# Fourteen steps of a two-part cached attention kernel written as a hardware loop of seven iterations

## Chip, cores and metric

The kernel runs on one core of a Trainium2 chip. The metric is the time of one execution in microseconds (us), as the device measures it. Several runs are made and their median is given.

## What is computed

Two attentions over a cache, A and B, each for one new token and 32 heads of 128 numbers, with 16384 cached positions per head. A looks at all positions, B only at the last 4096. Each multiplies its result by an output matrix, and the two results are put side by side.

```python
def _A_ref(x, k_cache, v_cache, wq, wo):      # B: the same over the last W = 4096 positions
    q = (x @ wq).reshape(B, Sq, Hq, Dh)       # one query row per head, 32 heads of 128
    scores = einsum("bhqd,bhkd->bhqk", q, k) * (Dh ** -0.5)
    p = softmax(scores)
    o = einsum("bhqk,bhkd->bhqd", p, v)
    return o.reshape(B, Sq, Hq * Dh) @ wo     # 4096 numbers times a 4096 x 512 matrix
...
return concatenate([a, b], axis=-1)
```

Nearly all bytes are the two caches: 352.32 MB are read from HBM in one execution.

## The kernel before, in words

**Steps.** The work is cut into 20 steps, and each step handles one tile of K and one tile of V. A tile is 128 partitions of 256 positions of 128 bf16 numbers, 8.39 MB. A step of A takes two heads (64 partitions each). A step of B takes two groups of four heads, loaded as two halves. There are 16 steps of A and 4 of B; B stands at the steps 0, 7, 13 and 19. A Python loop (`for T in range(NT)`, L446 and on) writes all 20 steps out one after the other, so the program is straight-line code.

**What a step does.** Scores are made on DVE: the K tile is multiplied by the query in place (`scores_prod`, L227), halves of the products are added until eight numbers per position are left (`scores_tree`, L233), and these are reduced (L237). That is done for both halves of the tile, and then `unit_max` takes the maximum (L244), which PE transposes into PSUM (L249). The rest of a step's work is done inside the next step, between its DVE instructions: `max_all` (DVE L262 and L264, PE L268), the exponentials on ACT (`soft`, L276 and L282; `spread_p`, L297), their sum on PE (L315), the product with V on PE (`pv`, 64 matmuls of 512 columns, L331), scaling on ACT (`evict`, L340), four small matmuls (`columns`, L348), and a copy into the collected output by ACT (L352).

**Buffers.** Two slots hold K tiles (`kring`) and one slot holds V tiles (`vring`). So the load of V for step T-1 can start only when the matmuls of `pv` of step T-2 have read the slot, and the load of K for step T+1 only when DVE has finished step T-1.

**Order.** `manual_schedule` keeps the instructions of each engine in the order in which they are written. All loads of K, V and the weights are issued by SP, in this order within step T: V of step T-1 (L132 for A, L141 for B), then K of step T+1 (L117 for A, L123 for B). An issue that has to wait holds up the issues behind it. The tail after the last step loads the second half of the last V tile and the output weights of B in five pieces (L141, L157), projects A's output (L383) and then B's (L397).

Of the kernel before, what the change touches and what calls it, by code (L numbers as in the profile page):

```python
# [11 lines left out]
P = 128  # L12
# [13 lines left out]
def kernel(  # L26
# [24 lines left out]
    singles = ctx.enter_context(tc.tile_pool(name="singles", bufs=1))  # L51
    kring = ctx.enter_context(tc.tile_pool(name="kring", bufs=2))
    vring = ctx.enter_context(tc.tile_pool(name="vring", bufs=1))
    small = ctx.enter_context(tc.tile_pool(name="small", bufs=3))
# [3 lines left out]
    ps_o = ctx.enter_context(tc.tile_pool(name="ps_o", bufs=1, space=bass.MemoryType.PSUM))  # L58
    ps_m = ctx.enter_context(tc.tile_pool(name="ps_m", bufs=2, space=bass.MemoryType.PSUM))

    def kslot(name):
        return kring.tile([P, 2 * CH, DH], BF16, tag="kring", name=name)

    def vslot(name):
        return vring.tile([P, 2 * CH, DH], BF16, tag="vring", name=name)

# [24 lines left out]

    steps, na, nb = [], 0, 0
    for T in range(HQ // 2 + HQ // 8):
        if T in (0, 7, 13, 19):
            steps.append((B, nb))
            nb += 1
        else:
            steps.append((A, na))
            na += 1
    NT = len(steps)  # L100
    assert na == HQ // 2 and nb == HQ // 8

    K, V = {}, {}

    def b_window(cache, g):
        return cache[0, 4 * g : 4 * g + 4, SkB - WB : SkB, :].rearrange("h (i l) d -> i h (l d)", l=CH)

    def a_pair(cache, g):
        return cache[0, 2 * g : 2 * g + 2, :, :].rearrange("h (i l) d -> (h i) l d", l=2 * CH)

    def new_k(T):
        K[T] = kslot("kt")

    def load_k(T, u=None):
        s, g = steps[T]
        if s is A:
            nc.sync.dma_start(  # L117
                out=K[T][:, :, :].rearrange("p l d -> p (l d)"),
                in_=a_pair(A_k_cache, g).rearrange("p l d -> p (l d)"),
            )  # L120
        else:
            for v in (0, 1) if u is None else (u,):
                nc.sync.dma_start(  # L123
                    out=K[T][:, v * CH : (v + 1) * CH, :].rearrange("p l d -> p (l d)"),
                    in_=b_window(B_k_cache, 2 * g + v),
                )

    def load_v(T):
        s, g = steps[T]
        V[T] = vslot("vt")  # L130
        if s is A:
            nc.sync.dma_start(  # L132
                out=V[T][:, :, :].rearrange("p l d -> p (l d)"),
                in_=a_pair(A_v_cache, g).rearrange("p l d -> p (l d)"),
            )
        else:
            for u in (0, 1):
                load_v_half(T, u, V[T][:, u * CH : (u + 1) * CH, :])

    def load_v_half(T, u, dst):  # L140
        nc.sync.dma_start(  # L141
            out=dst.rearrange("p l d -> p (l d)"), in_=b_window(B_v_cache, 2 * steps[T][1] + u)
        )

# [63 lines left out]

    class Unit:
        def __init__(self, T):  # L210
            self.T = T
            self.s, self.g = steps[T]
            self.n = 2 * CH // self.s.parts
            self.rows = 4 * self.s.nh
            self.last = T == NT - 1
            self.sc = one.tile([P, 2 * CH], F32, tag="sc", name="sc")

        def col(self, v):
            return self.s.nh * (self.s.parts * self.g + v)

    units = {}

    def scores_prod(T, u):
        s, g = steps[T]
        k = K[T][:, u * CH : (u + 1) * CH, :]
        j = g if s is A else 2 * g + u
        nc.vector.tensor_tensor(out=k, in0=k, in1=s.q[:, j : j + 1, :].broadcast_to([P, CH, DH]), op=ALU.mult)  # L227

    def scores_tree(T, u):
        k = K[T][:, u * CH : (u + 1) * CH, :]  # L230
        w = DH // 2
        while w >= 8:
            nc.vector.tensor_tensor(out=k[:, :, 0:w], in0=k[:, :, 0:w], in1=k[:, :, w : 2 * w], op=ALU.add)  # L233
            w //= 2
        if u == 0:
            units[T] = Unit(T)
        nc.vector.tensor_reduce(  # L237
            out=units[T].sc[:, u * CH : (u + 1) * CH], in_=k[:, :, 0:8], axis=AX.X, op=ALU.add
        )

    def unit_max(un):
        n = un.s.parts
        m = small.tile([P, 2], F32, tag="m", name="m")
        nc.vector.tensor_reduce(  # L244
            out=m[:, 0:n], in_=un.sc[:, :].rearrange("p (v l) -> p v l", v=n), axis=AX.X, op=ALU.max
        )
        un.sm = ps_m.tile([P, 512], F32, tag="sm", name="sm")
        for v in range(n):
            nc.tensor.transpose(un.sm[0:1, v * P : (v + 1) * P], m[:, v : v + 1], identf[:, :])  # L249
# [75 lines left out]
    def pv(un):  # L325
        s, n, G = un.s, un.n // 4, un.s.groups
        for i in range(n):
            for v in range(s.parts):
                r0 = 32 * (v * G + i % G)
                l = v * n + i  # L330
                nc.tensor.matmul(  # L331
                    s.o[r0 : r0 + un.rows, :],
                    lhsT=un.pm[:, l, :, :].rearrange("p a b -> p (a b)"),
                    rhs=V[un.T][:, 4 * l : 4 * l + 4, :],
                    start=(i < G), stop=(i >= n - G),
                )
# [5 lines left out]
    def columns(un):  # L342
        s = un.s
        w = s.parts * s.nh
        oc = ps_s.tile([P, 8], F32, tag="sp", name="oc")
        sel = s.sel[:, :, :].rearrange("k v (h c) -> k c (v h)", c=4)
        for j in range(4):
            nc.tensor.matmul(  # L348
                oc[:, 0:w], lhsT=un.osb[:, j * P : (j + 1) * P], rhs=sel[:, j, :],
                start=(j == 0), stop=(j == 3),  # L350
            )
        nc.scalar.copy(s.O[:, un.col(0) : un.col(0) + w], oc[:, 0:w])  # L352

    def pv_columns(un, v, V_t):
        s = un.s
        oc = ps_s.tile([P, 4], F32, tag="sp", name="ocol")
        for l in range(un.n):
# [4 lines left out]
        nc.vector.tensor_tensor(  # L362
            out=s.O[:, un.col(v) : un.col(v) + s.nh], in0=oc[:, :],
            in1=un.r[:, v * s.nh : (v + 1) * s.nh], op=ALU.mult,
# [25 lines left out]
    def project_out_columns(s, pieces):  # L390
# [19 lines left out]
        nc.sync.dma_start(out=out[0, 0, DN : 2 * DN].rearrange("(c f) -> c f", c=nf), in_=rows[:, :])  # L410

    wo_pieces = (16, 8, 4, 3, 1)
    with tc.manual_schedule():
        scratch = kslot("scratch")
        x0 = 4 * KC * P
        for s in (B, A):
            s.x_row = scratch[0:1, :, :].rearrange("p a b -> p (a b)")[:, x0 : x0 + D]
            for a, b in ((0, D // 4), (D // 4, D // 2), (D // 2, D)):
                nc.scalar.dma_start(out=s.x_row[:, a:b], in_=s.x[0, 0:1, a:b])  # L419
            x0 += D  # L420
        new_k(0)
        wqt = vslot("wqt")
        load_wq(B, wqt[:, 0:CH, :])
        load_k(0, 0)
        load_wq(A, wqt[:, CH : 2 * CH, :])
        load_k(0, 1)
        make_identity(nc, identf[:, :])
# [5 lines left out]
        nc.vector.tensor_copy(ident[:, :], identf[:, :])  # L433
        spread_x(B, scratch[:, :, :].rearrange("p a b -> p (a b)"))
        for s in (B, A):
# [7 lines left out]
        project_q(A)  # L443
        new_k(1)
        load_k(1)
        for T in range(NT):  # L446
            if T >= 1:
                load_v(T - 1)
                if T + 1 < NT:
                    new_k(T + 1)  # L450
                    load_k(T + 1)
            if T == NT - 1:
                W = kslot("wot")
                load_wo(A, W[:, 0:CH, :], (HQ,))
                load_v_half(T, 0, W[:, CH : 2 * CH, :])
            scores_prod(T, 0)
            if T >= 1:
                un = units[T - 1]
                max_all(un)
                soft(un)  # L460
                spread_p(un)
                soft_sum(un)
                pv(un)
            scores_tree(T, 0)
            if T >= 1:
                recip(un)
                evict(un)
                columns(un)
            scores_prod(T, 1)
            scores_tree(T, 1)  # L470
            if T < NT - 1:
                unit_max(units[T])
        Z = vslot("wot")
        load_v_half(NT - 1, 1, Z[:, 0:CH, :])
        load_wo(B, Z[:, CH : 2 * CH, :], wo_pieces)
        un = units[NT - 1]
        permute_o(A)
        project_out_rows(A)
# [7 lines left out]
        pv_columns(un, 0, W[:, CH : 2 * CH, :])  # L486
        pv_columns(un, 1, Z[:, 0:CH, :])
        permute_o(B)
# [31 lines left out]
```

## Time and profile before

| | us |
|---|---|
| median of 3 runs (825.7 to 826.01) | 825.76 |
| span of the profiled execution | 823.9 |
| outside the span (difference to the median) | 1.9 |
| DVE busy in the span | 763.9 (93%) |
| PE busy, matmuls | 202.7 (25%) |
| ACT busy | 60.1 (7%) |
| DMA queue q1, share of 16 engines | 99.2% |
| bytes read from HBM | 352.32 MB, 428 GB/s over the span |

The span is one profiled execution from the first instruction to the last. A share of busy time tells how much of the span an engine worked. It does not tell that the engine sets the end: that is read from the waits and from the chain of work that ended last. The DMA share is the mean over the 16 DMA engines that carry this core's transfers, counted as the time that their packets took. The line numbers of the rows are those of the kernel before.

### The profile page before, as it was taken

To read this page: it belongs to the slowest core of one execution; us is meant where nothing else is said; L and a number is where in the kernel's file an instruction comes from. 1 tells how busy PE (TensorE), PEld (TensorE's weight loads), DVE (VectorE), ACT (ScalarE), POOL (GpSimd) and SP (SyncE) were. 2 spreads that over 40 slices of the span, in tenths; PEclk is the share of its full clock that TensorE was granted. 3 is DMA by queue.
4 is the path that set the end of the run, shared out by engine and by line. 5 is a ranking of instruction groups with operands and counts; after the bars stand their busy time and mean duration, and the time that the engine had idled before them with its cause. 6 is when DMAs were issued, how large, how long until landed. Compare 5 with 4: busy or idle time off the path is not lost.

```text
span 823.9 us, 4724 instructions
## 1 busy us (share of the span) xinstructions
PE 202.7 (25%) x1985; PEld 100.7 (12%) x1985; DVE 763.9 (93%) x353; ACT 60.1 (7%) x168; POOL 0.7 (0%) x6
## 2 busy tenths in 40 slices
PE   2702212203030303130312213030303020303175
PEld 0201100101010101010101101010101010101035
DVE  2899999999999999999999999999999999999980
ACT  0101000001010000100000000010100000000010
POOL 0000000000000000000000000000000000000000
PEclk9865656565565555565555565565656565556585
DMA  9999999999999999999999999999999999999997
GB/s 384 434 433 433 453 420 443 430 436 440 423 446 420 424 439 443 412 453 420 443 417 449 414 452 410 450 417 428 438 449 424 436 433 430 443 414 445 418 429 296
DMA packets 8107, 352.62 MB, mean 428 GB/s; under 512 B 915, under 2 KB 1046, under 8 KB 1302
## 3 DMA queue, kind: packets, MB, share of 16 engines
q1 hardware_dynamic: 8072, 352.33, 99.2%
q8 instruction: 15, 0.25, 0.1%
q14 instruction: 6, 0.05, 0.0%
q10 hardware_dynamic: 14, 0.00, 0.0%
HBM read 352.32 MB, written 0.00 MB: 428 GB/s over the span
## 4 chain that ended last, share of the span: by engine, by line
DMA 82%; PE 15%; DVE 1%; SPq 0%; issue 0%; ACTq 0%; ACT 0%; DVEq 0%
DMA vt<-in_A_v_cache_dram 65%; DMA vt<-in_B_v_cache_dram 13%; PE oA L331 11%; DMA wot<-in_B_wo_dram 4%; PE oB L331 2%; PE qp L203 2%; DMA scratch<-in_A_x_dram 2%; DVE kt L227 1%; SPq L141 0%; ACTq L419 0%; SPq L157 0%; PE out_cols L397 0%; ACT qB L207 0%; PE out_rows L407 0%; DVE rows L409 0%
## 5 line engine op out<-in xcount | busy, mean ns | idle before, releaser
L233 DVE TENSOR_TENSOR kt<-kt 128x8192 bf16<-128x8192 bf16 (+3 forms) x160 | 344.9, 2156 | 4.8
L227 DVE TENSOR_TENSOR kt<-kt,qA 128x16384 bf16<-128x16384 bf16 x32 | 277.8, 8683 | 11.0 <-DMA kt<-in_A_k_cache_dram 10.9
L331 PE MATMUL oA<-vt,pm 128*8 128x512 bf16 x1024 | 92.3, 538 | 132.1 <-DMA vt<-in_A_v_cache_dram 132.1
L227 DVE TENSOR_TENSOR kt<-kt,qB 128x16384 bf16<-128x16384 bf16 x8 | 69.4, 8680 | 6.3 <-ACT qB L207 6.3
L249 PE MATMUL sm<-identf,m 128*1 128x128 f32 x24 | 8.1, 370 | 227.3 <-DVE m L244 227.3
L331 PEld LDWEIGHTS <-pm 128*8 128x8 bf16 (+1 forms) x1216 | 37.3, 111 | 216.7 <-issue 196.3
L268 PE MATMUL sm<-one_f,Mr 1*128 1x1 f32 x48 | 12.9, 347 | 176.7 <-DVE Mr L264 147.1
L237 DVE TENSOR_REDUCE sc<-kt 128x128 f32<-128x1024 bf16 x40 | 48.8, 1220 | 2.7
L276 ACT ACTIVATE bias<-sm 128x1 f32<-128x1 f32 (+1 forms) x20 | 3.4, 172 | 420.8 <-PE sm L268 420.8
L268 PEld LDWEIGHTS sm<-one_f,Mr 1*128 1x128 f32 x48 | 11.2, 298 | 183.6 <-DVE Mr L264 152.2
L249 PEld LDWEIGHTS sm<-identf,m 128*1 128x1 f32 x24 | 1.7, 79 | 229.3 <-issue 216.2
L340 ACT ACTIVATE o<-oA,r 128x512 f32<-128x512 f32 x16 | 11.0, 688 | 220.5 <-PE oA L331 220.5
L331 PE MATMUL oB<-vt,pm 128*16 128x512 bf16 x192 | 17.2, 494 | 20.3 <-DMA vt<-in_B_v_cache_dram 16.2
L348 PE MATMUL oc<-selA,o 128*128 128x2 f32 x128 | 16.9, 254 | 12.7 <-ACT o L340 12.7
L348 PEld LDWEIGHTS oc<-selA,o 128*128 128x128 f32 x128 | 15.5, 191 | 20.8 <-ACT o L340 20.8
L297 ACT ACTIVATE pm<-p,maskA 128x256 bf16<-128x256 bf16 x32 | 14.5, 500 | 0.5
L315 PE MATMUL sm<-cs,rowsA 128*128 128x1 f32 x32 | 9.4, 362 | 14.3 <-ACT p L282 14.3
L282 ACT ACTIVATE p<-sc,bias 128x256 bf16<-128x256 f32 (+1 forms) x24 | 11.3, 470 | 0.6
L203 PE MATMUL qp<-wqt,xbA 128*128 128x512 bf16 x32 | 8.8, 444 | 6.0 <-DVE kt L227 6.0
L315 PEld LDWEIGHTS sm<-cs,rowsA 128*128 128x128 f32 x32 | 8.0, 310 | 15.7 <-ACT p L282 15.7
L203 PE MATMUL qp<-wqt,scratch 128*128 128x512 bf16 x32 | 9.9, 486 | 0.0
L362 DVE TENSOR_TENSOR OB<-ocol,r 128x4 bf16<-128x4 f32 x2 | 0.3, 161 | 10.2 <-PE ocol L358 10.2
(71 smaller groups left out, 108.1 us busy)
## 6 DMA issues: line engine op xcount, KB each, us to landing
kt<-in_B_k_cache_dram SPq DMA_DIRECT2D x8, 4096.0 KB, 29.1
vt<-in_B_v_cache_dram SPq DMA_DIRECT2D x6, 4096.0 KB, 23.3
wot<-in_B_v_cache_dram SPq DMA_DIRECT2D x2, 4096.0 KB, 22.6
wqt<-in_B_wq_dram SPq DMA_DIRECT2D x1, 4096.0 KB, 12.3
wqt<-in_A_wq_dram SPq DMA_DIRECT2D x1, 4096.0 KB
wot<-in_A_wo_dram SPq DMA_DIRECT2D x1, 4096.0 KB
wot<-in_B_wo_dram SPq DMA_DIRECT2D x1, 2048.0 KB
wot<-in_B_wo_dram SPq DMA_DIRECT2D x1, 1024.0 KB
```

What stands on the lines that cost most here:

```text
L203: nc.tensor.matmul(qp[:, :, :], lhsT=s.xb[:, j, c, :], rhs=wq[:, c, j, g : g + 4, :], start=(k == 0), stop=(k == n - 1),)
L227: nc.vector.tensor_tensor(out=k, in0=k, in1=s.q[:, j : j + 1, :].broadcast_to([P, CH, DH]), op=ALU.mult)
L233: nc.vector.tensor_tensor(out=k[:, :, 0:w], in0=k[:, :, 0:w], in1=k[:, :, w : 2 * w], op=ALU.add)
L237: nc.vector.tensor_reduce(out=units[T].sc[:, u * CH : (u + 1) * CH], in_=k[:, :, 0:8], axis=AX.X, op=ALU.add)
L249: nc.tensor.transpose(un.sm[0:1, v * P : (v + 1) * P], m[:, v : v + 1], identf[:, :])
L268: nc.tensor.matmul(un.sm[:, 256 + v : 257 + v], lhsT=Mr[:, v * P : (v + 1) * P], rhs=one_f[:, :], start=True, stop=True,)
L282: nc.scalar.activation(out=un.p[:, v * n : (v + 1) * n], in_=un.sc[:, v * n : (v + 1) * n], func=ACT.Exp, scale=inv, bias=bias[:, v : v + ...
L297: nc.scalar.activation(out=out, in_=in_, func=ACT.Copy, scale=mask)
L315: nc.tensor.matmul(un.sm[v * w : (v + 1) * w, 264:265], lhsT=s.rows[:, :, :, :].rearrange("p r a b -> p (r a b)"), rhs=un.cs[:, v : v + 1] ...
L331: nc.tensor.matmul(s.o[r0 : r0 + un.rows, :], lhsT=un.pm[:, l, :, :].rearrange("p a b -> p (a b)"), rhs=V[un.T][:, 4 * l : 4 * l + 4, :], ...
L340: nc.scalar.activation(out=un.osb[:, :], in_=un.s.o[:, :], func=ACT.Copy, scale=un.r[:, 0:1])
L348: nc.tensor.matmul(oc[:, 0:w], lhsT=un.osb[:, j * P : (j + 1) * P], rhs=sel[:, j, :], start=(j == 0), stop=(j == 3),)
```

## The change

The order of the tiles becomes: tile 0 of B, all sixteen tiles of A, then the tiles 1, 2 and 3 of B. A function `step(prev, un, nxt)` holds one step. Step 0, step 1, and the steps 16 to 19 are written out as before. The fourteen steps 2 to 15 become a loop in the hardware, `tc.For_i`, with seven iterations of two steps. In it the number of the tile is a register, from which the addresses in HBM and the columns of the query and of the output are worked out. The tiles are no longer drawn from rings but fixed: two for K, one for V, one for the scores, two in PSUM for the transposed maxima. The copy of a step's output (`keep`) moves from ACT, where it stood behind the small matmuls, to DVE, where it stands at the end of the step.

```diff
-    kring = ctx.enter_context(tc.tile_pool(name="kring", bufs=2))
-    vring = ctx.enter_context(tc.tile_pool(name="vring", bufs=1))
+    slots = ctx.enter_context(tc.tile_pool(name="slots", bufs=1))
...
+    KS = [slots.tile([P, 2 * CH, DH], BF16, tag=f"k{i}", name=f"k{i}") for i in range(2)]
+    VS = slots.tile([P, 2 * CH, DH], BF16, tag="v", name="v")
+    SC = slots.tile([P, 2 * CH], F32, tag="sc", name="sc")
+    SM = [ps_m.tile([P, 512], F32, tag=f"sm{i}", name=f"sm{i}") for i in range(2)]
...
-        if T in (0, 7, 13, 19):
-            steps.append((B, nb))
...
     def a_pair(cache, g):
-        return cache[0, 2 * g : 2 * g + 2, :, :].rearrange("h (i l) d -> (h i) l d", l=2 * CH)
+        heads = cache[0, bass.ds(2 * g, 2), :, :]
+        return heads.rearrange("h (i l) d -> (h i) l d", l=2 * CH).rearrange("p l d -> p (l d)")
...
-        nc.vector.tensor_tensor(out=k, in0=k, in1=s.q[:, j : j + 1, :].broadcast_to([P, CH, DH]), op=ALU.mult)
+        nc.vector.tensor_tensor(
+            out=k, in0=k, in1=s.q[:, bass.ds(j, 1), :].broadcast_to([P, CH, DH]), op=ALU.mult
+        )
...
-        nc.scalar.copy(s.O[:, un.col(0) : un.col(0) + w], oc[:, 0:w])
+        un.oc = oc[:, 0:w]
+
+    def keep(un):
+        nc.vector.tensor_scalar_mul(un.ocol(0, un.s.parts * un.s.nh), un.oc, 1.0)
...
+    def step(prev, un, nxt, tail=None):
+        if prev is not None:
+            load_v(prev)
+            if nxt is not None:
+                load_k(nxt)
+        if tail is not None:
+            tail()
+        scores_prod(un, 0)
+        if prev is not None:
+            max_all(prev)
+            soft(prev)
+            spread_p(prev)
+            soft_sum(prev)
+            pv(prev)
+        scores_tree(un, 0)
+        if prev is not None:
+            recip(prev)
+            evict(prev)
+            columns(prev)
+        scores_prod(un, 1)
+        scores_tree(un, 1)
+        if prev is not None:
+            keep(prev)
+        if not un.last:
+            unit_max(un)
...
+        order = [(B, 0)] + [(A, g) for g in range(NA)] + [(B, g) for g in range(1, NB)]
+        units = [Unit(s, g, T % 2, T == NT - 1) for T, (s, g) in enumerate(order)]
...
+        step(None, units[0], None)
+        step(units[0], units[1], units[2])
+        with tc.For_i(0, NA - 2, 2, iteration_sync="reg_based") as g:
+            for j in (0, 1):
+                step(Unit(A, g + j, (1 + j) % 2), Unit(A, g + j + 1, j % 2), Unit(A, g + j + 2, (1 + j) % 2))
+        for T in range(NA, NT):
             if T < NT - 1:
-                unit_max(units[T])
...
+                step(units[T - 1], units[T], units[T + 1])
```

In the program that is built from it, the body of the loop ends on each engine with a compare-and-branch back to the body's start. The waits inside the body compare semaphores with registers that are advanced once per iteration. Behind the loop stands one block that is passed once: SP waits for the last transfers and instructions of the loop, then all five engines meet at a barrier, GpSimd clears the loop's semaphores, and each engine branches to the code behind the loop.

## Prediction

> **What bounds the kernel now.** I read the page's engine shares and queues first, then the chain that ended last, then the waits of DVE and of the DMA queue, and last the timeline of one step.
>
> ```profile
> PE 202.7 (25%) x1985; PEld 100.7 (12%) x1985; DVE 763.9 (93%) x353; ACT 60.1 (7%) x168; POOL 0.7 (0%) x6
> ...
> q1 hardware_dynamic: 8072, 352.33, 99.2%
> q8 instruction: 15, 0.25, 0.1%
> ...
> DMA 82%; PE 15%; DVE 1%; SPq 0%; issue 0%; ACTq 0%; ACT 0%; DVEq 0%
> ```
>
> DVE is busy 93% of the time, but the DMA engines 99.2%, and the chain runs 82% over transfers. The PE part of the chain is `pv`, behind which V's slot comes free. DVE, the second busiest, is slightly faster than the transfers:
>
> ```profile
> DVE kt L227 <- DMA kt<-in_A_k_cache_dram: 10.9, 15, 1.4
> ```
>
> In 15 of 16 steps of A, DVE waits for its K tile, 10.9/15 = 0.73 us each time. V lands every 38.8 us in the chain (237.30, 276.01, 314.82), which is 2 x 8.39 MB at 432 GB/s. DVE's own work is about 38.1 us a step. One boundary between steps shows how far ahead the queue is filled:
>
> ```profile
> 255.78 0.42 DVE L244 TENSOR_REDUCE m<-sc 128x1 f32<-128x256 f32 x1
> 256.68 8.69 DVE L227 TENSOR_TENSOR kt<-kt,qA 128x16384 bf16<-128x16384 bf16 x1 [0.48 <-DMA kt<-in_A_k_cache_dram]
> ```
>
> ```profile
> 256.34 0.37 PE L249 MATMUL sm<-identf,m 128*1 128x128 f32 x1 [11.74 <-DVE m L244]
> 265.86 0.58 PE L268 MATMUL sm<-one_f,Mr 1*128 1x1 f32 x2 [9.15 <-DVE Mr L264]
> ```
>
> ```profile
> 242.80 0.33 SPq L132 DMA_DIRECT2D vt<-in_A_v_cache_dram  x1
> 255.77 1.19 SPq L123 DMA_DIRECT2D kt<-in_B_k_cache_dram  x2
> 282.62 0.33 SPq L132 DMA_DIRECT2D vt<-in_A_v_cache_dram  x1
> ```
>
> When K lands at 256.6, the next V has been queued for 13.8 us (242.80), and the next K for 0.9 us, with 19.4 us of V ahead of it. So V's issue may come 13 us late and K's 19 us late before the DMA engines stand idle. That cover decides the rest: a delay on SP, PE or ACT below it costs nothing, and DVE has 0.73 us a step of its own.
>
> **The loop's body, at each turn.** The listing of the built program has no barrier and no drain there, only register operations, a compare and a branch. What each engine pays:
> - SP: four issues per turn, each behind a register operation. The cover is 13 us; I count 0.
> - PE: it idles 9.15 us between L249 and L268 around each boundary, 11.74 us before L249. A branch that has to fetch code is hidden there. The body is some 280 instructions, twice the 128 matmuls and loads of `pv` and more. The page has 15 instruction packets of 0.25 MB for 3970 loads and matmuls, 265 each, so a turn may ask for one or two packets again. By the row they took 0.1% of 16 x 823.9 us, some 13 us, 0.9 us each, on one of 16 engines. Between 7 fewer and 8 more packets, spread over 16 engines, that is -0.4 to +0.5 us of transfer time. I take +0.2.
> - ACT loses the copy of L352 (0.16 us); it has 7% of work; 0.
> - DVE: `keep` adds one instruction per step. The nearest row is the reciprocal of 0.16 us (L323), whose successor starts 0.08 us after it; I take 0.1. Its input is ready: V lands about 20 us into the step, `pv` and what follows end 10 us later, and `keep` stands at 38 us. The waits against registers need a register operation ahead of each; it can run while the instruction before is at work, so 0, at worst the 0.07 us by which a separate wait delays L237 (starts 34 ns behind its producer without one, 103 ns with one). The compare and branch overlap the last reduction (L244, 0.42 us) or not: 0 to 0.3 us a turn. DVE's slack per turn is 2 x 0.73 = 1.46 us; 0.2 + 0.2 goes, and 1 us is left. DVE still waits for K at every step, and the loop runs at the speed of the transfers: 0.
>
> **The exit, once.** Here SP waits until the K tile for step 16 has landed, then all engines meet. Only afterwards is V of step 15 issued, which the old order issued 13 us earlier. The DMA engines have nothing queued in between, and what they lose is lost. The bubble in pieces:
> - the last packet's end to the wait's release: at the tail the last packet of the trace ends at 820.05 and its landing is at 820.19: 0.15 us.
> - SP's last wait and drain, the meeting, the clearing, the release: the same sequence ends this program.
>
> ```profile
> L515 SPq EVENT_SEMAPHORE  x7: 17/28/28, 822.3 to 823.8; - x7
> L515 POOLq EVENT_SEMAPHORE  x4: 17/17/17, 823.2 to 823.8; - x4
> ```
>
> From SP's last wait (823.07 in the trace) to its release from the first barrier (823.35) 0.28 us pass; the second barrier, with the clearing, ends at 823.83, 0.48 later. One barrier with a clearing is 0.5 us by these.
> - the branch, register operations and two waits before the issue: 60 ns from one SP wait to the next in that sequence, so 0.2 us.
> - issue to full flow: the first load is issued at 0.73, and in the windows of the first microseconds the share of the DMA engines reads so:
>
> ```profile
> 0.00:1.00 1.00, 0.00 (x0) 0.00 (x0) 0.13 (x3) 0.00 (x0) 0.41 (x5) 1.00 0.00 0
> 1.00:2.00 1.00, 0.00 (x0) 0.00 (x0) 0.92 (x3) 0.00 (x0) 0.29 (x1) 1.00 1.06 295
> 2.00:3.00 1.00, 0.00 (x0) 0.00 (x0) 0.85 (x3) 0.18 (x1) 0.00 (x0) 1.00 0.70 229
> 3.00:4.00 1.00, 0.00 (x0) 0.00 (x0) 0.24 (x1) 1.00 (x1) 0.00 (x0) 1.00 1.06 459
> ```
>
> The last column is GB/s: 983 KB by 4.0 us, which full rate (432) carries in 2.28 us. Of the 3.27 us since the issue 1.0 is lost.
> - the other engines at the barrier: DVE's maximum ends 0.7 us before K lands, PE's transpose 0.5 us after that maximum; with `keep` they arrive together with K. I take 0.1; up to 0.5 if DVE runs late.
>
> The sum is 0.15 + 0.5 + 0.2 + 1.0 + 0.1 = 1.95. The 16 engines start up to 1.1 us apart (first packets at 1.75 to 2.88), of which the byte count averages away about half; I add 0.3. The bubble is 2.25 us, between 1.6 (barrier 0.3, nothing late) and 3.5 (all starts late, PE late by 0.5).
>
> [...]
>
> **The order of the tiles.** B's steps 7 and 13 move to 17 and 18. In the chain, V of B lands after the same 38.8 us (353.62, 586.14), and bytes are equal: 0. At the tail `pv` of step 18 is B's: 5.1 to 5.3 us against 6.5, so the last loads (787.87) are issued 1.2 us earlier. The queue still holds 8.39 MB then: 0.
>
> **Sum.** 823.9 + 0.2 + 2.25 = 826.3, and 1.9 outside the span: 828.2 us, 0.3% over the median.
>
> **Rivals.**
> 1. *DVE becomes the bound inside the loop.* If every one of about 34 waits of a turn loses 0.07 us, that is 2.4 us, with `keep` and the branch 2.8, against 1.46 of slack: 1.3 us a turn, 9 us over seven turns. The transfers have 19 us of cover, but the exit collects the lag: 828.2 + 9 = 837. It decides from 30 ns per wait. Against it: register operations wait for nothing.
> 2. [...]
> 3. *Not slower.* PE's code stays on the core through all turns: 7 packets fewer. If the slowest DMA engine, which alone decides when a tile has landed, served two of them, it gains 1.8 us and repays a bubble at its lower end of 1.6: 825.6. It decides from two packets on that engine. Against it: nothing in the page says which engine carries them.
>
> **How the numbers follow.** This measurement can tell about 0.2%, 1.65 us, from no change, that is 824.1 to 827.4. Forecast, one bubble (827.0 to 829.5): 66%, some of it below 827.4. DVE bound (830 to 838): 14%. Code stalls or hidden barriers (838 to 850): 7%. Not slower (824.1 to 827): 11%. Faster than that, by something the profile doesn't show: 2%. Leaving out the stalls and half of the not slower leaves 826.4 to 837. Slower by over 0.2%: 0.77, within: 0.20, faster: 0.03.
>
> **What would show it.** Right: one gap of about 2 us in the transfers between the landing of the K tile of step 16 and the next V issue, some 645 us in; V landing every 38.8 us before and after it; DVE waiting about 0.6 us for K in each turn. Rival 1: no wait for K in the loop, gaps of 100 ns between DVE's instructions, a longer gap at the exit. [...] Rival 3: clearly fewer instruction packets on q8. I would be wrong if the loop's issues took SP longer than the cover, or if addresses from registers made the transfers themselves slower.

## The result

The changed kernel takes 830.9 us (830.4 to 831.03, 4 runs), beside 825.87 us of the kernel before in the same comparison: 5.0 us more, ratio 1.006 with a 95% interval of 1.0047 to 1.0074. The forecast was 828.2, 2.4 us more. The direction was right and the time lies in the range (826.4 to 837), but the loss is twice what was worked out. The span of the profiled execution is 829.2 us, 5.3 more than before.

The page of the kernel after, with the rows that answer to those shown of before (engine shares, then queues with packets, MB and share of 16 engines):

```profile
PE 201.3 (24%) x1985; PEld 101.0 (12%) x1985; DVE 764.6 (92%) x372; ACT 57.0 (7%) x149; POOL 0.7 (0%) x6
...
q1 hardware_dynamic: 8072, 352.33, 98.7%
q8 instruction: 8, 0.13, 0.1%
```

The same bytes now take 98.7% of a longer span: the DMA engines stood idle somewhere. q8 carries 8 packets of code instead of 15. DVE has 19 more instructions (`keep`) and 0.7 us more work. Its waits and one boundary between steps inside the loop:

```profile
DVE k L203 <- DMA k<-in_A_k_cache_dram: 9.5, 15, 2.0
```

```profile
257.65 0.15 DVE L330 TENSOR_SCALAR OA<-oc 128x2 f32 x1
257.77 0.42 DVE L220 TENSOR_REDUCE m<-sc 128x1 f32<-128x256 f32 x1
258.79 8.69 DVE L203 TENSOR_TENSOR k<-k,qA 128x16384 bf16<-128x16384 bf16 x1 [0.60 <-DMA k<-in_A_k_cache_dram]
```

DVE still waits 9.5/15 = 0.63 us for each K tile, so the transfers set the pace in the loop as they did before. `keep` (L330) delays the next instruction by 0.12 us.

**Where the 5 us are.** The product with V starts as soon as a V tile has landed (0.04 us behind it in the chain of before), so its first matmul is a clock for the transfers. Undisturbed, two such starts are 38.72 us apart. The timeline of PE in the kernel before and then in the kernel after (start, duration, instruction, idle time before it), at steps 1 to 3 and 15 to 17:

```profile
81.08 5.04 PE L331 MATMUL oB<-vt,pm 128*16 128x512 bf16 x63 [5.30 <-DMA vt<-in_B_v_cache_dram]
120.77 5.66 PE L331 MATMUL oA<-vt,pm 128*8 128x512 bf16 x64 [8.14 <-DMA vt<-in_A_v_cache_dram]
159.75 4.96 PE L331 MATMUL oA<-vt,pm 128*8 128x512 bf16 x64 [8.14 <-DMA vt<-in_A_v_cache_dram]
...
626.01 5.63 PE L331 MATMUL oA<-vt,pm 128*8 128x512 bf16 x64 [8.14 <-DMA vt<-in_A_v_cache_dram]
665.00 4.92 PE L331 MATMUL oA<-vt,pm 128*8 128x512 bf16 x64 [8.14 <-DMA vt<-in_A_v_cache_dram]
703.70 6.04 PE L331 MATMUL oA<-vt,pm 128*8 128x512 bf16 x64 [8.13 <-DMA vt<-in_A_v_cache_dram]
```

```profile
81.51 5.98 PE L306 MATMUL oB<-v,pm 128*16 128x512 bf16 x63 [5.30 <-DMA v<-in_B_v_cache_dram]
123.11 5.67 PE L306 MATMUL oA<-v,pm 128*8 128x512 bf16 x64 [9.51 <-DMA v<-in_A_v_cache_dram]
161.81 5.10 PE L306 MATMUL oA<-v,pm 128*8 128x512 bf16 x64 [8.14 <-DMA v<-in_A_v_cache_dram]
...
626.53 6.53 PE L306 MATMUL oA<-v,pm 128*8 128x512 bf16 x64 [8.13 <-DMA v<-in_A_v_cache_dram]
668.76 5.91 PE L306 MATMUL oA<-v,pm 128*8 128x512 bf16 x64 [11.04 <-DMA v<-in_A_v_cache_dram]
708.34 4.04 PE L306 MATMUL oA<-v,pm 128*8 128x512 bf16 x47 [12.48 <-DMA v<-in_A_v_cache_dram]
```

The first line of each belongs to step 0, of B, whose V comes in two halves; the start of the second half is shown. Subtract the starts before from those after, and then one difference from the next:

| stretch | lag at its end, us | added, us |
|---|---|---|
| up to 81 | 81.51 - 81.08 = 0.4 | +0.4 |
| entry of the loop | 161.81 - 159.75 = 2.1 | **+1.6** (+1.9 in its first step) |
| the twelve starts inside | 626.53 - 626.01 = 0.5 | **-1.5** |
| exit of the loop | 708.34 - 703.70 = 4.6 | **+4.1** (+3.2 in its first step) |
| the rest | 829.2 - 823.9 = 5.3 | +0.7 |

There are two bubbles, not one, and a gain between them. The windows show the exit's: the last columns are the share of the DMA engines and GB/s, first of the kernel before, then after. A packet counts in the window in which it starts, so the row of after says that none starts in these 3 us, not that none is under way:

```profile
643.00:646.00 3.00, 0.37 (x1) 0.08 (x1) 2.19 (x4) 0.00 (x0) 0.00 (x0) 0.50 1.06 459
```

```profile
643.00:646.00 3.00, 0.37 (x1) 0.08 (x1) 2.36 (x4) 0.00 (x0) 0.00 (x0) 0.50 0.00 0
```

The packets of the trace place it exactly: no data packet runs from 645.41 to 647.46. A second hole, with one packet at work in place of 16 from 100.38 and none from 101.68 to 102.1, stands where the loop is entered. The waits of SP (the DMA queue's own) and its timeline there say whom it waited for:

```profile
SPq L130 <- PEq L452: 38.1, 1, 38.1
```

```profile
61.44 0.33 SPq L120 DMA_DIRECT2D k<-in_A_k_cache_dram  x1
101.10 0.37 SPq L130 DMA_DIRECT2D v<-in_A_v_cache_dram  x1
101.82 0.34 SPq L120 DMA_DIRECT2D k<-in_A_k_cache_dram  x1
```

L452 is the line of the loop, and PEq is PE's sequencer. Behind the K issue of 61.44 SP waits for PE at the loop's head. The V slot is free at 87.5, but V is issued at 101.10. On reaching the loop PE adds to its own loop semaphore (at 100.76 in the trace), and SP's first wait inside, on that semaphore, ends at 100.84. PE reaches the loop behind the transpose of step 1's maximum, which starts at 100.77 behind DVE's last instruction of that step. So the entry makes SP wait for the end of step 1.

### The profile page after: what moved, and what is told of

Read it like the earlier page. It is cut to its first block, busy times and chain, and to the rows that moved or that the text cites. A ratio compares the mean times of both kernels' runs of the same rounds, so it can differ in the third digit from the quotient of the medians.

```text
span 829.2 us, 5319 instructions
## 1 busy us (share of the span) xinstructions
PE 201.3 (24%) x1985; PEld 101.0 (12%) x1985; DVE 764.6 (92%) x372; ACT 57.0 (7%) x149; POOL 0.7 (0%) x6
## 3 DMA queue, kind: packets, MB, share of 16 engines
q1 hardware_dynamic: 8072, 352.33, 98.7%
## 5 line engine op out<-in xcount | busy, mean ns | idle before, releaser
L211 DVE TENSOR_TENSOR k<-k 128x8192 bf16<-128x8192 bf16 (+3 forms) x160 | 344.9, 2156 | 4.8
L203 DVE TENSOR_TENSOR k<-k,qA 128x16384 bf16<-128x16384 bf16 x32 | 277.8, 8682 | 10.5 <-DMA k<-in_A_k_cache_dram 9.5
L306 PE MATMUL oA<-v,pm 128*8 128x512 bf16 x1024 | 89.3, 525 | 136.9 <-DMA v<-in_A_v_cache_dram 136.9
L203 DVE TENSOR_TENSOR k<-k,qB 128x16384 bf16<-128x16384 bf16 x8 | 69.4, 8680 | 5.8 <-ACT qB L197 5.5
L213 DVE TENSOR_REDUCE sc<-k 128x128 f32<-128x1024 bf16 x40 | 48.8, 1220 | 3.5 <-DVE k L211 0.5
L306 PE MATMUL oB<-v,pm 128*16 128x512 bf16 x192 | 18.6, 532 | 31.1 <-DMA v<-in_B_v_cache_dram 29.7
L193 PE MATMUL qp<-v,xbA 128*128 128x512 bf16 x32 | 9.8, 479 | 6.6 <-DMA v<-in_A_wq_dram 6.6
L237 DVE TENSOR_REDUCE M<-sm 1x2 f32<-1x128 f32 (+1 forms) x20 | 6.0, 299 | 5.2 <-PE sm L224 5.2
```

Of the source, the lines that this page charges most:

```text
L193: nc.tensor.matmul(qp[:, :, :], lhsT=s.xb[:, j, c, :], rhs=wq[:, c, j, g : g + 4, :], start=(k == 0), stop=(k == n - 1),)
L203: nc.vector.tensor_tensor(out=k, in0=k, in1=s.q[:, bass.ds(j, 1), :].broadcast_to([P, CH, DH]), op=ALU.mult)
L213: nc.vector.tensor_reduce(out=un.sc[:, u * CH : (u + 1) * CH], in_=k[:, :, 0:8], axis=AX.X, op=ALU.add)
L306: nc.tensor.matmul(s.o[r0 : r0 + un.rows, :], lhsT=un.pm[:, l, :, :].rearrange("p a b -> p (a b)"), rhs=VS[:, 4 * l : 4 * l + 4, :], start ...
```

## The experiments

The theory after the result: the loop costs its two ends and nothing else, the entry through PE's late arrival, the exit through the drained queue; inside, fewer packets of code give a part back. Six kernels test it. All comparisons are with the kernel before, on the same chip as the experiment; the kernel with one loop of seven was not run again there, and its 830.9 stands beside 825.87 of the kernel before, which took 825.83 and 825.72 in the experiments.

**1. No loop, all else of the change.**

```diff
-        with tc.For_i(0, NA - 2, 2, iteration_sync="reg_based") as g:
-            for j in (0, 1):
-                step(Unit(A, g + j, (1 + j) % 2), Unit(A, g + j + 1, j % 2), Unit(A, g + j + 2, (1 + j) % 2))
+        for T in range(2, NA):
+            step(units[T - 1], units[T], units[T + 1])
```

> The changed kernel with its hardware loop written out as fourteen steps of straight-line code; order of the tiles, fixed tiles and the copy on DVE stay. Theory (the time is lost at the two ends of the loop, 2.8 us of transfer time where it is entered and 3.2 us where it is left): both gaps go, time 825.9 within 0.5 us, no gap in the transfers between 10 and 800 us. Rival (the new order of the tiles, or the copy on DVE, costs part of it): over 827 us.

Measured 825.70 against 825.83, ratio 0.9999 (0.999 to 1.0008), and no gap in the packets. The order of the tiles, the fixed tiles and the copy on DVE cost nothing that can be measured.

**2. Two turns in place of seven.** Steps 2 to 11 are written out and the loop runs from 10 to `NA - 2`.

> The loop has two iterations (steps 12 to 15) in place of seven; steps 2 to 11 are written out. Theory (the cost is one entry and one exit, whatever the number of turns): the same two gaps, one of them now shortly before step 12 at about 490 us; time 831 to 832 us, a little above the kernel with seven turns, since more code is fetched. Rival (a cost in each turn): 5.0 x 2/7 = 1.4 us over the kernel before, 827.3 us.

Measured 831.51, ratio 1.007 (1.0056 to 1.0083). Gaps without any packet stand at 488.8 and 646.4 us and nowhere else. The entry's step takes 511.03 - 469.95 = 41.08 us, the exit's 42.62, beside 38.72 undisturbed. So two turns cost what seven cost, but for 0.6 us (831.51 beside 830.9), with 14 packets on q8 in place of 8.

**3. PE reaches the loop earlier.** The transposes move into a function that the next step calls ahead of `max_all`; the two maxima get fixed tiles.

```diff
-        for v in range(n):
-            nc.tensor.transpose(un.sm[0:1, v * P : (v + 1) * P], m[:, v : v + 1], identf[:, :])
+    def turn_max(un):
+        for v in range(un.s.parts):
+            nc.tensor.transpose(un.sm[0:1, v * P : (v + 1) * P], un.m[:, v : v + 1], identf[:, :])
...
         if prev is not None:
+            turn_max(prev)
             max_all(prev)
```

> The transposes of a step's maxima on PE stand at the head of the next step in place of the end of their own, so PE reaches the head of the loop when it is done with step 0's product with V, and not only after DVE's last instruction of step 1. Theory (the first V issue inside the loop waits until PE has arrived at the loop): that issue comes 13 us earlier, at about 88 us, the gap at 100 us goes with its 2.8 us, the gap at the exit stays; time 828.1 us, within 0.6. Rival (the gap at the entry comes from code that is fetched or from SP's own jump into the loop): 830.9 us as before, with the gap.

Measured 828.84, ratio 1.0042 (1.0028 to 1.0055; one of the five runs took 830.54, the others 828.71 to 829.16): 2.1 us of the 5 are gone, less than the 2.8 expected by 0.7, and the time misses its margin of 0.6 by 0.1. SP's timeline and the starts of the product around the entry in this kernel:

```profile
60.95 0.34 SPq L122 DMA_DIRECT2D k<-in_A_k_cache_dram  x1
87.92 0.36 SPq L132 DMA_DIRECT2D v<-in_A_v_cache_dram  x1
100.06 0.34 SPq L122 DMA_DIRECT2D k<-in_A_k_cache_dram  x1
```

```profile
81.03 5.74 PE L310 MATMUL oB<-v,pm 128*16 128x512 bf16 x63 [5.30 <-DMA v<-in_B_v_cache_dram]
121.17 6.15 PE L310 MATMUL oA<-v,pm 128*8 128x512 bf16 x64 [8.00 <-DMA v<-in_A_v_cache_dram]
```

V is issued at 87.92, and the hole at 100 us is gone. The step that held it takes 121.17 - 81.03 = 40.14 us in place of 41.60; in the kernels without a loop it takes 39.7 to 40.1. What remains is the exit: 42.38 and then 39.69 us between starts, 4.6 us over two undisturbed steps. The 2.8 were too high a count: by the packets of the kernel after, the 16 engines stood idle for 2.1 us on average around the entry (99.5 to 103.5 us). The entry's price in time is 1.5 us by this step, 1.6 by the table, 2.1 by the medians of this run, and 2.4 by its step in experiment 2 (41.08 - 38.72): some 2 us.

**4. Two loops behind each other** (`for lo, hi in ((0, 6), (6, NA - 2))` around the loop).

> Two loops of three and four iterations directly behind each other in place of one of seven. Theory (an exit costs 3.2 us; an entry costs only what PE's arrival delays the first V issue, and behind an exit all engines arrive together): three gaps, the new one at about 335 us like that of the exit; time 830.9 + 3.2 = 834.1 us, up to 835 if the second entry adds some. Rival (entry and exit each cost their price wherever they stand): 830.9 + 6.0 = 836.9 us.

Measured 838.31, ratio 1.0151 (1.0137 to 1.0164), 7.4 us above one loop: more than both. The rival has the better number, for another reason. Between the loops no data packet runs for 3.5 us (335.40 to 338.91), 1.5 us longer than at the single exit. After the barrier releases SP at 336.35, SP needs until 337.95 to issue V: four additions to semaphores, five register moves, a branch, a hint and the waits stand in its way, where 0.15 us pass behind a plain exit. At the first entry this head was hidden, since SP had worked it off while it waited for PE (61.82 to 62.63 us in the kernel after; released at 100.84 there, it issued V at 101.10). The starts of the product around the boundary:

```profile
316.52 5.56 PE L306 MATMUL oA<-v,pm 128*8 128x512 bf16 x64 [8.13 <-DMA v<-in_A_v_cache_dram]
359.81 6.10 PE L306 MATMUL oA<-v,pm 128*8 128x512 bf16 x64 [10.77 <-DMA v<-in_A_v_cache_dram]
400.05 6.46 PE L306 MATMUL oA<-v,pm 128*8 128x512 bf16 x64 [8.14 <-DMA v<-in_A_v_cache_dram]
```

43.29 + 40.24 - 2 x 38.72 = 6.1 us for one boundary, of which 1.5 are the head and the rest is an exit. Some 1.3 of the 7.4 us stay unexplained. In the profiled execution, where the span is 6.8 us longer than with one loop, 1.0 us of it stands behind the last product (43.8 us to the end in place of 42.8).

**5. A barrier in every turn** (`iteration_sync="barrier"`).

> The changed kernel with a full barrier at the end of every iteration in place of waits against registers: SP waits for all transfers of the iteration, all engines meet, the semaphores are cleared. It shows what each turn of the loop was spared. Theory (a bubble of the kind found at the exit costs 3.2 us of transfer time wherever it stands): six more of them, 830.9 + 6 x 3.2 = 850 us, with seven gaps 77.5 us plus a bubble apart. Rival (the bubble is mostly hidden behind DVE's work, and the exit's price had another source): under 840 us.

Measured 852.2, ratio 1.0322 (1.0306 to 1.0338). The mode has no bubble at the entry (its step takes 121.14 - 81.08 = 40.06 us, as in the kernels without a loop), and seven bubbles 81.4 us apart: 26.5/7 = 3.8 us each. The starts of the product around the first of them:

```profile
159.85 4.89 PE L306 MATMUL oA<-v,pm 128*8 128x512 bf16 x64 [8.13 <-DMA v<-in_A_v_cache_dram]
202.48 5.75 PE L306 MATMUL oA<-v,pm 128*8 128x512 bf16 x64 [10.66 <-DMA v<-in_A_v_cache_dram]
241.20 5.17 PE L306 MATMUL oA<-v,pm 128*8 128x512 bf16 x64 [8.16 <-DMA v<-in_A_v_cache_dram]
```

The step with the bubble takes 42.63 us, 3.9 over 38.72, and the one behind it 38.72 again; so it is at all six bubbles inside the loop (3.8 to 4.0, then 0.0), where 2.7 to 2.8 us pass without a data packet. Only behind the exit does the second step take longer too (39.82). The price per drained queue is near that of the exit (4.1), some more than the 3.2 that the theory took. Waits against registers spare six of them (830.9 us in place of 852.2).

**6. More code, no loop.** In the kernel before, behind `columns`:

```diff
         nc.scalar.copy(s.O[:, un.col(0) : un.col(0) + w], oc[:, 0:w])
+        for j in range(64):
+            nc.tensor.matmul(un.sm[:, 400:401], lhsT=ident[:, :], rhs=ident[:, 0:1], start=True, stop=True)
```

> The kernel before, with 64 small matmuls more per step on PE, written to an unused PSUM column while PE has nothing to do; they add 2432 loads and matmuls to the straight-line code and no transfer of data. Theory (each packet of instructions holds one of the 16 DMA engines and costs 0.1 us of transfer time on average, which is what the loop saves inside): 9 to 10 packets more, 25 in place of 15 on q8, 1.0 us slower, 826.8. Rival (packets are free): 825.8.

Measured 827.47 against 825.72, ratio 1.0024 (1.0014 to 1.0034), 1.75 us for ten packets:

```profile
q1 hardware_dynamic: 8072, 352.33, 99.0%
q8 instruction: 25, 0.41, 0.2%
```

```profile
626.33 5.05 PE L331 MATMUL oA<-vt,pm 128*8 128x512 bf16 x64 [8.13 <-DMA vt<-in_A_v_cache_dram]
666.56 5.41 PE L331 MATMUL oA<-vt,pm 128*8 128x512 bf16 x64 [8.14 <-DMA vt<-in_A_v_cache_dram]
```

More code costs time, but 0.17 us a packet is only an average. Between 121 and 783 us 17 steps of this kernel hold packets of q8, and 15 of them take 38.72 us to within 0.1. Two take 40.2: the one shown (packet at 633.1) and the one from 353.58 to 393.80 (packet at 357.9). It is not the extra matmuls as such: they stand in every step, and long steps occur without them. In the kernel before one step takes 39.8 us (586.18 to 626.01, packet at 590.1), and experiment 1, with the other order of the tiles, has 39.84 us at the same place with a packet at the same time. Inside the loop of the kernel after, where PE runs the same body of some 310 loads and matmuls in every turn and no packet of q8 comes between 130 and 640 us, no step takes over 38.82. So in these kernels every long step away from the loop's ends holds a packet, though most packets lengthen nothing, and the 1.5 us that the loop gave back are 1.1 of that one step and 0.4 of small ones. Why a few packets cost 1.1 to 1.5 us and most cost nothing no run shows; the packets of the trace do not say which engine carried them.

No version of the loop beats the kernel before. The best, experiment 3, keeps the exit.

## Why the prediction was right and where it failed

- *The transfers bound the kernel, with 0.7 us of slack on DVE.* Right: DVE waits for K in the loop as before (0.63 us), and the loop's turns cost nothing.
- *DVE pays nothing for waits against registers.* Right. The gap between dependent instructions is 34 ns in the loop too (only ahead of L213 it grew, by 7 ns in the mean); the register operation runs while the instruction before is at work (the one ahead of `keep` from 256.53 to 256.62, during L213's 256.51 to 257.73). Rival 1 falls with this and with experiment 2, and so do code stalls or barriers at every turn (no step inside the loop takes over 38.82 us).
- *The order of the tiles, the copy on DVE.* 0 by experiment 1, as forecast.
- *One bubble at the exit, 2.25 us.* The mechanism was right, the size too small. The pieces until the first packet held, but for the landing: 645.41 to 645.85 from the last packet to SP's wait (0.44; forecast 0.15), 0.50 for the barrier (645.85 to 646.35; 0.5), 0.14 to the issue (0.2), 0.97 from the issue to the first packet (1.0). That sums to 2.05 us without a packet, close to the 1.95 of the forecast.
- *The landing, 0.15 us.* This was a wrong pair: the packet that ends at 820.05 belongs to the last piece of the output weights, and the landing at 820.19 is that of the piece before it. The last piece landed at 820.51, 0.46 us behind its packet, and the exit's tile 0.43 us (645.41 to 645.84).
- *The 16 engines apart, 0.3 us.* Here the bubble was undersized, in what lies around the hole: packets stop one after the other and start one after the other (644.9 to 645.4, 647.5 to 648.5), and the tile behind the gap waits for the last. The six bubbles inside the loop of experiment 5, with no code packet near them, show it by itself: 3.8 to 4.0 us for 2.7 to 2.8 without a packet, so some 1.1 where the forecast took 0.3. The exit's first step lost 3.5 against 38.72 us (3.2 against the kernel before). The 0.9 us of the second step seem to have another source, code that is fetched behind the loop: where a packet of code stands in the second step behind a drained queue (672.5 here), it took 0.5 to 1.5 us longer in five cases; where none stands there, 0.1 at the last exit of experiment 4 and 0.0 at the six bubbles inside the loop of experiment 5. That is read from the traces side by side; no run tested it.
- *SP's issues inside the loop: "The cover is 13 us; I count 0".* This is the step that failed. It holds for every turn but the first. The working did not ask what the first V issue inside waits for. It waits for PE to arrive, and V is issued 13.6 us after the slot is free (87.5 to 101.1), just beyond the cover. The prediction had named this as a sign of being wrong (issues that take SP longer than the cover), without a price. Experiment 3 shows the cause by taking it away. Worth some 2 us.
- *Code packets, +0.2.* They gave some 1.5 us back. Rival 3 had the mechanism (7 fewer, and a few of them that count in full), with a gain of 1.8; that the slowest engine served those few fits its condition but is not shown.
- *The time in the range.* In part luck. 830.9 lies outside the 827.0 to 829.5 given to one bubble and inside the 830 to 838 given to a DVE bound, which is not what happened. An entry at 0, an exit too small by some 2 us and a gain that was left out (1.5) partly offset each other.

The sum with the measured terms: 0.4 + 1.6 - 1.5 + 4.1 + 0.7 = 5.3 us of span. The 0.4 before the loop and the 0.7 behind it are not traced to a cause.

## What to carry to other kernels

Where transfers set the pace, price a hardware loop at its two ends (here some 2 us and 4.1), not at its turns: find out at which instruction each engine reaches the head and who waits there for it, and count a drained queue at the exit. Let the engine whose arrival is awaited have nothing late in front of the loop; moving the transposes behind the loop's head brought 2.1 us. Two ends cost the same for two turns as for seven (831.51 and 830.9 us) and a second loop behind the first 7.4 us more, so short loops and loops in series were the worst trade.

## What the runs showed that was not expected

- A drained and refilled queue cost 3.5 to 4.0 us in the step that held it, though only 2.05 (exit) to 2.8 us (experiment 5) pass without a packet.
- A packet of 16 KB of code took some 1.1 us. Of such packets most cost the kernel nothing, and a few cost 1.1 to 1.5 us.
- A loop's head cost SP 1.5 us between release and first issue when nothing hid it.
